# A spectral mixing and ELU kernel: the opening of batch 0 gets own output tiles, fewer early rows and a re-dealt weight conversion

## The chip, the cores and the metric

The kernel runs on one core of a Trainium2 chip. The core has five engines that run their own instruction streams and meet at semaphores: PE (TensorE, matrix multiply), DVE (VectorE), ACT (ScalarE), POOL (GpSimd) and SP (SyncE, which here issues most of the DMAs). The metric is the device time of one launch in microseconds (us).

## The reference

```python
# x (8, 3008, 256), filters (1505, 256), w_in (256, 2048), w_out (2048, 256)
X = np.fft.rfft(x, axis=1)
Y = X * (filt_r + 1j * filt_i)[None]
y = np.fft.irfft(Y, n=3008, axis=1).astype(np.float32)
t = y.reshape(8 * 3008, 256)              # 24064 tokens
h = t @ w_in
g = np.where(h > 0, h, np.exp(np.minimum(h, 0)) - 1)
out = (g @ w_out).astype(np.float32)
```

The two weights and only they come as float64; the kernel makes float32 of them on the chip.

## The kernel before, in words

**Mixing.** 3008 = 47 x 64, so each transform is done as two factors with twiddles inside the tables. Per batch, a first factor (`a_unit`, or `a_first` for batch 0), a second factor with the product by the filter and its inverse (`b_unit`, `bi_unit`; in batch 0 `b_first`, `bi_first`), and a last factor that delivers tokens (`n_unit`, and `n_first` for the first tile of batch 0). Between the second factor and the last the rows pass through a DRAM buffer: `y_write` (`y_write_first`) writes them, `y_read` (`y_read_first`) reads them in another order.

**The two dense layers.** There are 8 x 6 x 4 = 192 items (batch b, token tile m, quarter q of the 2048 hidden columns). An item is 14 up matmuls (`up_steps`, line 592, and the ELU on ACT and DVE) and 14 down matmuls (`down_steps`, line 675); the 2 x 2 block product is done in 7 products, with sums of weight blocks (`w_sums`) and of data blocks (`n_sums`) made ahead. The downs of an item run between the ups of the next. The order of every engine's stream is written by hand: `plan` holds, for a (quad, place) key, what is done in which of five gaps of the loop over items. Batch b+1's mixing units lie in the gaps of batch b's items. Batch 0 runs its items in the order (tile 0: q0, q1), (tile 1: q0 to q3), (tile 0: q2, q3).

**The opening** is what comes before the first item. DMAs bring x, tables, the filter and the first weights (SP in order, some on POOL). `a_first` runs for six x pieces; then for eight tiles g, `t_first` transposes, `b_first` multiplies, DVE makes four `products` with the filter (tile `ff`), and two tiles later `bi_first` does the inverse factor; ACT copies its result from PSUM (lines 388 and 389) into the tile `t3f` for g up to 5, two buffers in turn, and into `t2` for g of 6 and 7. `y_write_first` then sends it to DRAM, 24 rows each. So the copy of tile 2 goes where tile 0's result lies, and has to wait until tile 0's four DMAs have read it. After tile 7 dummy matmuls (`warm`, 5 of them, line 945) run on PE while the rows go out and come back (`y_read_first`, 406) for `n_first` (543). A short burst of such matmuls (3) also stands at the very start.

**Weight conversion.** There are 16 blocks k of 512 float64 values per partition (four per quarter: k%4 of 0 and 1 are w_in, 2 and 3 are w_out). `w_fetch` loads one; `w_split` is two integer operations on DVE (lines 777, 778), `w_float` three activations on ACT (787), `w_join` two more DVE operations (795, 798) and the multiply that writes the weight (802 for w_in, 808 twice for w_out); `w_sums` is four operations on half as many elements, on POOL for most k and on DVE for 13 and 15 (814 to 817). In the opening and in the first six quads these stand between the other work, by the tables `BESIDE` and `early`. An item of quarter q needs the blocks and sums of its quarter before its up or down matmuls.

**Batch 1's first factor** needs sums and differences of x (`x_unit`, 226 and 227): for batch 1 all six pieces on POOL, from batch 2 on DVE. `f_arrange` puts the filter into a DRAM copy `fp`, which `f_read` (POOL's DMA queue, 348) reads per tile; `z_read` and `z_write` pass the first factor's result through DRAM.

Of the kernel before, what the change touches and what calls it, by code (L numbers as in the profile page):

```python
# [37 lines left out]
XSUMS = 6  # L38
WTMP = (0, 1, 0, 1, 0, 1, 2, 3, 0, 2, 3, 2, 3, 2, 3, 2)
# [98 lines left out]
def kernel(  # L138
# [185 lines left out]
    def z_read(b, g):  # L324
        t = t2[:, g % 2]
        for p in range(4):
            k = p * K2 + 4 * g
            nc.sync.dma_start(t[32 * p:32 * p + 24].rearrange("i u d -> i (u d)"),
                              zs[b][:, k:k + 4, :].rearrange("i u d -> i (u d)"))

    def f_read_first(g0, g1, a, queue):

        r = slice(64 * a, 64 * a + 48)
        w0, w1 = 1 if g0 == a == 0 else 0, 2 * (g1 - g0)
        k = 16 * a + 2 * g0
        for c, src in enumerate((filt_r, filt_i)):
            t = ff[r, c, g0:g1].rearrange("p g u d -> p (g u) d")
            queue.dma_start(t[0:48:2], raw(src, k, [[64 * D, 24], [D, w1], [1, D]]))
            for j, n in ((0, 16), (16, 7)):
                queue.dma_start(t[1 + 2 * j:2 * (j + n):2, w0:w1],  # L340
                                raw(src, 64 * (j + 1) - k - w0, [[64 * D, n], [-D, w1 - w0], [1, D]]))
            if w0:
                queue.dma_start(t[1:48:2, 0], raw(src, 32, [[64 * D, 24], [1, D]]))

    def f_read(b, g):
        t = fbufs[g % 2]
        for a in range(4):
            nc.gpsimd.dma_start(t[32 * a:32 * a + 24].rearrange("p c u d -> p (c u d)"),  # L348
                                fp[g, a].rearrange("q c u d -> q (c u d)"))
# [28 lines left out]
    def bi_first(g):  # L378
        s = ss.pop((0, g))
        t = t3s[0, g] = (t2 if g > 5 else t3f)[:, g % 2]  # L380
# [14 lines left out]
    def y_write_first(g, i0=0, i1=24):  # L395
        if g == 0:
# [115 lines left out]
    def n_unit(b, m):  # L512
        t, w, h = t4s.pop((b, m)), tns.pop((b, m)), half(m)
        ps = [bank(n) for n in ("pse", "pso")]
        for q, i in enumerate(order(m)):
            n = 32 if i == 0 else 64
            for dh in range(2):
                for o in (0, 64):
                    for (_, p), r in zip(ps, HALVES):
# [57 lines left out]
    def up_steps(b, m, q):  # L577
# [4 lines left out]
        for tag, names in G_TAGS:  # L582
            t = gp.tile([P, len(names), 2, 256], FP32, tag=tag, name=tag)
# [159 lines left out]
    def w_fetch(k, queue=nc.gpsimd):  # L743
# [4 lines left out]
        elif k in (9, 12):  # L748
            wd = t2[:, 1 if k == 12 else 0].rearrange("p u d -> p (u d)")
        elif k == 13:  # L750
            wd = t3s["first"][:, 0].rearrange("p u d -> p (u d)")
        elif k == 15:
            wd = op.tile([P, 16, 2, 32], FP32, tag="o", name="wd").rearrange("p j e s -> p (j e s)")
        else:
            wd = fbufs[{5: 0, 6: 1, 7: 2, 10: 0, 11: 1, 14: 2}.get(k, k)].rearrange("p c u d -> p (c u d)")
# [33 lines left out]
    def w_join(k, *parts):  # L789
# [3 lines left out]
        for part in parts or range(3):  # L793
# [5 lines left out]
            elif j < 2:  # L799
                a, b = (t.rearrange("p (a j c) -> p a j c", a=2, j=2) for t in (f, e.bitcast(FP32)))  # L800
                dst = w_in[q][:, 2 * j:2 * j + 2, :, :].rearrange("p j a c -> p a j c")
                nc.vector.tensor_tensor(out=dst, in0=a, in1=b, op=ALU.mult)
            else:

                a, b = (t.rearrange("p (i a e s) -> p i e a s", i=2, a=4, e=2) for t in (f, e.bitcast(FP32)))
                dst = w_out[q][:, 0:4, j - 2, :].rearrange("p (i e) (a s) -> p i e a s", i=2, a=4)
                for i in range(2):
                    nc.vector.tensor_tensor(out=dst[:, i], in0=a[:, i], in1=b[:, i], op=ALU.mult)
# [21 lines left out]

    with tc.manual_schedule():


        with tc.tile_pool(name="boot", bufs=1) as bp:
            ff = bp.tile([P, 2, NG, 2, D], FP32, name="ff")
            once = bp.tile([P, 2, P], FP32, name="once")
            eye, gf = once[:, 0], once[:, 1].rearrange("p (v q) -> p v q", v=2)
            gs = bp.tile([P, 3, 2, 64], FP32, name="gs")
            gr, gi = gs[:, 1], gs[:, 2]
# [5 lines left out]
            zt[0] += [bp.tile([P, 16 * ROWS], FP32, name="zt%d" % i) for i in range(2)]  # L845
# [3 lines left out]
            for k in range(3):  # L849
# [7 lines left out]
            for c in range(2):  # L857
                x_load_first(c)
            w_fetch(0, nc.sync)
            for c in range(2, 6):  # L860
                x_load_first(c)
                if c == 3:
                    w_fetch(1, nc.sync)
# [4 lines left out]
            for gh in range(2):  # L868
                nc.gpsimd.memset(ff[:, :, 4 * gh:4 * gh + 4], 0.0)
# [9 lines left out]

            f_read_first(0, 2, 0, nc.sync)  # L880
            f_read_first(0, 2, 1, nc.gpsimd)
            f_read_first(2, 4, 0, nc.sync)
            w_fetch(2, nc.sync)
            f_read_first(2, 4, 1, nc.gpsimd)
            f_read_first(4, 8, 0, nc.sync)
            f_read_first(4, 8, 1, nc.gpsimd)
            ta_first(0)
            ta_first(1)
            w_split(0)
            ta_first(2)  # L890
            ta_first(4)
            for c in range(NXC):
                a_first(c)
                if c == 2:
                    w_float(0)
            w_join(0)
            w_split(1)
            for k in (3, 4):
                w_fetch(k, nc.sync)
            w_fetch(5)  # L900
            t4f = xp.tile([P, 2, 2, D], FP32, tag="xc", name="t4f").rearrange("p k u d -> p (k u) d")
            w_fetch(8)
            t8 = tnp.tile([P, 4, P], FP32, tag="tn", name="t8")
            BESIDE = {0: ((w_float, 1, 0),), 1: ((w_split, 2), (w_float, 1, 1, 2)), 2: ((w_float, 2, 0), (w_join, 1, 0)),
                      3: ((w_join, 1, 1), (w_float, 2, 1, 2)), 4: ((w_join, 1, 2), (w_sums, 1, nc.gpsimd), (w_fetch, 6), (w_split, 3)),
                      5: ((w_join, 2, 0), (w_float, 3, 0)), 6: ((w_join, 2, 1), (w_float, 3, 1, 2)),
                      7: ((w_join, 2, 2), (w_fetch, 7)), 8: ((w_join, 3), (w_split, 4))}
            for g in range(2):
                t_first(g)
            for g in range(NG + 2):  # L910
                back = (lambda g=g: bi_first(g - 2)) if g >= 2 else None
                if g < NG:
                    b_first(g, (ff[:, 0, g], ff[:, 1, g]), pqs[g % 2], back)
# [4 lines left out]
                for fn, *a in BESIDE.get(g, ()):  # L918
                    fn(*a)
                if 2 <= g < NG:  # L920
                    y_write_first(g - 2)
                elif g >= NG:
                    y_write_first(g - 2, 0, 4)
                if g == 4:
                    nc.sync.dma_start(t8, t8_d)
                if g == NG:
                    y_read_first(0, 6)
            y_read_first(6, 8)
            for g in (6, 7):
                y_write_first(g, 4, 24)  # L930
            w_sums(3, nc.gpsimd)
            w_float(4)
            w_split(5)
            w_join(4)
            w_float(5)
            w_split(6)
            w_join(5)
            w_float(6)
            w_sums(5, nc.gpsimd)
            w_split(7)  # L940
            w_join(6)
            w_float(7)
            warm = psO.tile([P, 512], FP32, tag="po2", name="warm")
            for k in range(5):
# [5 lines left out]
        gp = pool("gp", 2)  # L950
        ep = pool("ep", 2)
        op = pool("op", 1)
        n_first(t8)
        tn_read(0, 1)
        y_read(0, 1)
        for k in (9, 10):
            w_fetch(k, nc.sync)
        for c in range(2):
            x_load(1, c)
        for k in (11, 12, 13, 15):  # L960
            w_fetch(k, nc.sync)
# [6 lines left out]
        def at(quad, place, fn, *a):  # L968
            plan.setdefault((quad, place), []).append((fn, a))


        early = ((0, 2, w_join, 7, 0, 1), (0, 2, w_split, 8), (0, 4, w_float, 8, 0), (0, 0, w_float, 8, 1, 2), (0, 0, w_join, 7, 2),
                 (0, 0, w_sums, 7, nc.gpsimd), (0, 3, n_unit, 0, 1), (0, 1, w_join, 8, 0, 1), (0, 1, w_split, 9), (0, 1, w_fetch, 14, nc.sync),
                 (1, 2, n_sums, 0, 1, 0, 1), (1, 2, w_float, 9, 0), (1, 4, n_sums, 0, 1, 2), (1, 0, w_join, 8, 2), (1, 0, w_float, 9, 1, 2),
                 (1, 0, w_split, 10), (1, 3, w_join, 9, 0, 1), (1, 1, w_join, 9, 2), (1, 1, w_sums, 9, nc.gpsimd), (1, 1, w_float, 10, 0),
# [136 lines left out]
```

## Time and profile before

| | us |
|---|---|
| median of 3 runs | 2577.06 (2576.66 to 2580.13) |
| the profiled execution | 2575.46 |
| its span, first to last instruction | 2573.7 |
| PE, DVE, ACT, POOL busy | 2529.4, 2071.6, 1528.2, 189.3 |
| first item's first matmul | 79.73 |
| third item of tile 1 done, seventh item begins | 173.41 |

The profiled execution is 1.6 us below the median. "First item" and "seventh item" are the first matmuls of line 592 of these items in the timeline. The span falls into three parts: the opening, with loads and the first tile's mixing; six items beside which most of the weights are converted; and the rest, about 2400 us, where PE is busy nearly all the time.

### The profile page before, as it was taken

What the parts mean: (1) busy time and instruction counts of PE and PEld (TensorE: products, weight loads), DVE (VectorE), ACT (ScalarE), POOL (GpSimd) and SP (SyncE); (2) the same over time, 40 slices, a digit from 0 to 9 for tenths busy, and PEclk for the clock granted to TensorE, in tenths of its full rate; (3) what the DMA queues carried; (4) which work ended last, traced back from release to release, by engine and by line L of the source; (5) the groups of instructions that cost most, each with busy time, mean ns of one, the idle gap of its engine ahead of it and who ended that gap; (6) DMA issues with size and microseconds to landing.
All of it is one profiled execution on the core that took longest, in us unless ns stands there. A gap on an engine that the chain in (4) does not pass through costs nothing.

```text
span 2573.7 us, 44194 instructions
## 1 busy us (share of the span) xinstructions
PE 2529.4 (98%) x16732; PEld 2160.7 (84%) x16732; DVE 2071.6 (80%) x3612; ACT 1528.2 (59%) x2698; POOL 189.3 (7%) x325
## 2 busy tenths in 40 slices
PE   8889999999999999999999999999999999999998
PEld 5678889888898888988889888888888888898887
DVE  4988887788877888788887888778887788876666
ACT  4665665666556555665556656565656665555554
POOL 3421100010000000000000000000010011000000
PEclk8999999999999999999999999999999999999999
DMA  8753213522234231433215231243213322110010
GB/s 209 207 146 76 68 23 84 138 69 56 48 87 123 56 74 44 113 83 74 61 40 143 71 81 36 72 124 82 56 48 80 85 62 68 36 46 19 19 28 17
DMA packets 229288, 196.38 MB, mean 76 GB/s; under 512 B 129050, under 2 KB 202748, under 8 KB 228980
## 3 DMA queue, kind: packets, MB, share of 16 engines
q1 hardware_dynamic: 215828, 167.62, 26.7%
q0 software_dynamic: 12096, 25.68, 3.5%
q8 instruction: 132, 2.16, 0.3%
q14 instruction: 80, 0.66, 0.1%
q10 hardware_dynamic: 1152, 0.26, 0.1%
HBM read 121.60 MB, written 74.97 MB: 76 GB/s over the span
## 4 chain that ended last, share of the span: by engine, by line
PE 88%; DVE 6%; ACT 2%; DMA 2%; issue 1%; SPq 0%; POOL 0%; DVEq 0%; POOLq 0%; ACTq 0%
PE po L675 41%; PE phs L592 23%; PE phd L592 12%; PE pha L592 6%; PE pse L520 2%; PE pf L419 1%; PE psa L240 1%; PE pv L485 1%; DVE g L600 1%; DVE g L614 1%; DMA ff<-in_filt_i_dram 1%; ACT e L610 1%; ACT e L609 1%; PE pso L520 0%; DMA x<-in_x_dram 0%
## 5 line engine op out<-in xcount | busy, mean ns | idle before, releaser
L675 PE MATMUL po<-g,wo 128*128 128x256 f32 (+1 forms) x5376 | 1316.8, 377 | 0.0
L675 PEld LDWEIGHTS po<-g,wo 128*128 128x128 f32 x5376 | 1013.5, 190 | 165.2 <-issue 49.4
L603 ACT ACTIVATE g<-phs 128x512 f32<-128x512 f32 (+1 forms) x576 | 338.6, 588 | 717.2 <-PE phs L592 716.1
L592 PE MATMUL phs<-y,wi 128*128 128x256 f32 (+1 forms) x2288 | 580.7, 376 | 1.5 <-DVE g L614 1.1
L610 ACT ACTIVATE e<-e 128x512 f32<-128x512 f32 (+1 forms) x768 | 477.1, 621 | 24.3
L592 PEld LDWEIGHTS phs<-y,wi 128*128 128x128 f32 x2288 | 430.5, 190 | 56.5 <-ACT g L603 1.8
L600 DVE TENSOR_TENSOR g<-phd,g 128x512 f32<-128x512 f32 (+1 forms) x384 | 258.9, 674 | 267.0 <-ACT e L610 196.8
L609 ACT ACTIVATE e<-g 128x512 f32<-128x512 f32 (+1 forms) x576 | 353.4, 614 | 66.3 <-DVE g L600 51.2
L614 DVE SCALAR_TENSOR_TENSOR g<-e,g 128x512 f32<-128x512 f32 (+1 forms) x576 | 387.8, 673 | 1.6 <-ACT e L610 0.9
L614 DVE SCALAR_TENSOR_TENSOR g<-e,phs 128x512 f32<-128x512 f32 (+1 forms) x192 | 129.7, 675 | 139.2 <-ACT e L610 139.2
L592 PE MATMUL phd<-y,wi 128*128 128x256 f32 (+1 forms) x768 | 196.3, 378 | 11.4 <-DVE g L600 11.4
L592 PE MATMUL phs<-ys,wi 128*128 128x256 f32 (+1 forms) x784 | 198.7, 376 | 6.4 <-ACT g L603 5.6
L592 PE MATMUL phd<-ys,wi 128*128 128x256 f32 (+1 forms) x768 | 193.8, 375 | 0.0
L592 PE MATMUL pha<-ys,wi 128*128 128x256 f32 (+1 forms) x752 | 190.0, 375 | 0.0
L609 ACT ACTIVATE e<-phs 128x512 f32<-128x512 f32 (+1 forms) x192 | 113.3, 590 | 113.2 <-PE phs L592 113.2
L592 PEld LDWEIGHTS phd<-y,wi 128*128 128x128 f32 x768 | 145.7, 191 | 32.2 <-DVE g L600 16.1
L592 PEld LDWEIGHTS phs<-ys,wi 128*128 128x128 f32 x784 | 147.6, 190 | 25.2 <-ACT g L603 7.8
L348 POOL DMA_DIRECT2D fall<-fp x224 | 110.0, 499 | 692.0 <-DVE r L458 686.4
L592 PEld LDWEIGHTS phd<-ys,wi 128*128 128x128 f32 x768 | 145.7, 190 | 16.6
L592 PEld LDWEIGHTS pha<-ys,wi 128*128 128x128 f32 x752 | 142.8, 190 | 16.5
L600 DVE TENSOR_TENSOR g<-pha,g 128x512 f32<-128x512 f32 (+1 forms) x192 | 129.0, 672 | 24.3 <-PE pha L592 24.3
L654 DVE TENSOR_TENSOR g<-g,g 128x512 f32<-128x512 f32 (+1 forms) x192 | 132.6, 690 | 6.6
(184 smaller groups left out, 2175.4 us busy)
## 6 DMA issues: line engine op xcount, KB each, us to landing
t<-yd SPq DMA_DIRECT2D x94, 256.0 KB
z<-t SPq DMA_DIRECT2D x84, 256.0 KB
fall<-fp POOLq DMA_DIRECT2D x224, 96.0 KB, 2.9
t<-z SPq DMA_DIRECT2D x224, 96.0 KB
yd<-t SPq DMA_DIRECT2D x112, 192.0 KB
out_dram<-o SPq DMA_DIRECT2D x632, 32.0 KB
xc<-in_x_dram SPq DMA_DIRECT2D x84, 128.0 KB
xc<-in_x_dram SPq DMA_DIRECT2D x161, 64.0 KB
```

The lines of the kernel that those rows point to most:

```text
L240: nc.tensor.matmul(p[o:o + 64, u, :], w[r, u, o:o + 64], src[r, u, :], start=True, stop=True)
L348: nc.gpsimd.dma_start(t[32 * a:32 * a + 24].rearrange("p c u d -> p (c u d)"), fp[g, a].rearrange("q c u d -> q (c u d)"))
L419: nc.tensor.matmul(pf[p][1][32 * a:32 * a + 32, js, :], fb[r, v, :], t2[r, js, a, :], start=True, stop=True, tile_position=(32 * p, 32 * a))
L520: nc.tensor.matmul(p[o:o + 64, dh, ds(64 * q, n)], t[r, i - 4 * m, ds(dh * P + o, 64)], w[r, i - 4 * m, 0:n], start=True, stop=True)
L592: nc.tensor.matmul(ps[:, a, 0:h], w_in[q][:, COMBO[n], a, :], y[n], start=start and a == 0, stop=True, skip_group_check=True)
L600: nc.vector.tensor_tensor(out=g[o], in0=i0, in1=i1, op=ALU.add)
L603: nc.scalar.activation(out=g[o], in_=i0, func=AXT.Copy)
L609: nc.scalar.activation(out=e, in_=src, func=AXT.Relu, scale=-1.0)
L610: nc.scalar.activation(out=e, in_=e, func=AXT.Exp, scale=-1.0)
L614: nc.vector.scalar_tensor_tensor(out=g[n], in0=es[n], scalar=1.0, in1=src, op0=ALU.subtract, op1=ALU.max)
L654: nc.vector.tensor_tensor(out=g["t4"], in0=g["b21"], in1=g["t2"], op=ALU.subtract)
L675: nc.tensor.matmul(po[i][:, u, 0:h], w_out[q][:, COMBO[n], a, :], g[n][:, a, :], start=begin and a == 0 and n in (1, 3, 6, 4), stop=True, ...
```

## The change

It has these parts. (1) The filter tile `ff` is split in `ff0` (real) and four tiles `ff1` (imaginary) that lie in the homes of `up_steps`' first g tiles of odd items and of the output tile; the even results of `bi_first` go into those `ff1` tiles, the odd ones into `t3f` and `t2`, so each of the eight results has its own home. POOL clears half as much, ACT clears `ff1`. (2) `y_write_first` sends only the first 8 rows in the opening (4 for tiles 6 and 7, then the other 4), and one `y_read_first` reads them all; rows 8 to 24 are sent during the first items (`early`). (3) The multiply of the conversion becomes `w_mult`, with the engine as an argument; 10 of 16 go to POOL. All conversion steps are single and stand in other places (`OPEN`, `early`); all `w_sums` are on POOL; fetches are all on SP, block 0 ahead of x. (4) `x_unit` of batch 1 runs on POOL for three pieces and on DVE for three. (5) `z_read` and `f_read` move two tiles in one DMA. (6) 6 instead of 3 dummy matmuls at the start and 11 instead of 5 before `n_first`. (7) `n_unit` issues each pair of matmuls in the other order.

```diff
-XSUMS = 6
-WTMP = (0, 1, 0, 1, 0, 1, 2, 3, 0, 2, 3, 2, 3, 2, 3, 2)
+XSUMS = 3
+WTMP = (0, 1, 0, 1, 0, 2, 1, 1, 0, 3, 3, 2, 3, 2, 3, 2)
...
     def bi_first(g):
         s = ss.pop((0, g))
-        t = t3s[0, g] = (t2 if g > 5 else t3f)[:, g % 2]
+        t = t3s[0, g] = outs_first[g]
...
-                    for (_, p), r in zip(ps, HALVES):
+                    for (_, p), r in reversed(tuple(zip(ps, HALVES))):
...
-            t = gp.tile([P, len(names), 2, 256], FP32, tag=tag, name=tag)
+            t = gps[(4 * m + q) % 2].tile([P, len(names), 2, 256], FP32, tag=tag, name=tag)
...
+    def w_mult(k, eng=nc.vector):
+        q, j = divmod(k, 4)
+        _, e, f = w_tmp(k)
+        if j < 2:
...
+            eng.tensor_tensor(out=dst, in0=a, in1=b, op=ALU.mult)
+        else:
...
+            for i in range(2):
+                eng.tensor_tensor(out=dst[:, i], in0=a[:, i], in1=b[:, i], op=ALU.mult)
...
-            ff = bp.tile([P, 2, NG, 2, D], FP32, name="ff")
+            ff0 = bp.tile([P, NG, 2, D], FP32, name="ff")
+            ff1 = [gps[0].tile([P, 2, 2, 256], FP32, tag="g%d" % (i + 1), name="ff") for i in range(3)]
+            ff1.append(op.tile([P, 16, 2, 32], FP32, tag="o", name="ff").rearrange("p (g u w) e s -> p g u (w e s)", g=2, u=2))
+            outs_first = [ff1[g // 2].rearrange("p g u d -> p (g u) d") if g % 2 == 0 else (t3f if g < 4 else t2)[:, g // 2 % 2]
+                          for g in range(NG)]
...
+            OPEN = {0: ((w_split, 1), (w_float, 1, 1, 2, 0),),
...
+                    7: ((w_split, 2), (w_float, 2, 1), (w_fetch, 3, nc.sync), (w_float, 2, 0),),
+                    8: ((w_join, 2, 1), (w_float, 2, 2), (w_join, 2, 0),),
+                    9: ((w_mult, 1, nc.vector), (w_mult, 2, nc.gpsimd),),
...
+                    11: ((w_fetch, 4, nc.sync),),
+                    12: ((w_split, 4), (w_fetch, 7, nc.sync), (w_split, 3),),
...
+                    17: ((w_mult, 3, nc.gpsimd), (w_fetch, 8, nc.sync), (w_split, 9), (w_split, 6), (w_float, 6, 0), (w_split, 5), (w_float, 5, 1, 0), (w_float, 6, 1), (w_join, 6, 1), (w_sums, 3, nc.gpsimd), (w_float, 6, 2),),
+                    18: ((w_join, 6, 0), (w_fetch, 11, nc.sync), (w_join, 5, 1), (w_mult, 6, nc.gpsimd), (w_float, 9, 0), (w_split, 7), (w_float, 5, 2), (w_join, 5, 0),),
+                    19: ((w_fetch, 12, nc.sync),)}
...
-                if 2 <= g < NG:
-                    y_write_first(g - 2)
-                elif g >= NG:
-                    y_write_first(g - 2, 0, 4)
+                conv(8 + g)
+                if g >= 2:
+                    y_write_first(g - 2, 0, 8 if g < NG else 4)
...
+        early = ((0, 2, w_mult, 5, nc.vector), (0, 2, y_write_first, 4, 8, 24), (0, 2, y_read, 0, 1), (0, 2, y_write_first, 6, 8, 24), (0, 2, w_float, 7, 0), (0, 2, y_write_first, 0, 8, 24),
+                 (0, 4, w_float, 7, 1), (0, 4, w_join, 7, 1), (0, 4, w_mult, 4, nc.gpsimd), (0, 4, w_fetch, 10, nc.sync), (0, 4, y_write_first, 2, 8, 24), (0, 4, x_load, 1, 1), (0, 4, w_split, 11), (0, 4, x_load, 1, 0), (0, 4, w_float, 7, 2), (0, 4, w_float, 9, 1),
+                 (0, 0, w_split, 8), (0, 0, x_load, 1, 2),
...
+                 (1, 2, w_float, 8, 1, 0), (1, 2, y_write_first, 5, 8, 24), (1, 2, w_mult, 7, nc.vector), (1, 2, w_float, 8, 2), (1, 2, x_unit, 1, 1), (1, 2, n_unit, 0, 1),
+                 (1, 0, w_join, 8, 0), (1, 0, x_unit, 1, 0), (1, 0, f_arrange, 1, 1), (1, 0, n_sums, 0, 1, 0, 1), (1, 0, w_sums, 7, nc.gpsimd),
...
+                 (4, 3, w_mult, 13, nc.gpsimd), (4, 3, f_arrange, 0, 1), (4, 3, w_mult, 12, nc.gpsimd),
+                 (4, 1, y_read, 0, 2), (4, 1, w_split, 15), (4, 1, w_sums, 11, nc.gpsimd), (4, 1, w_sums, 13, nc.gpsimd),
...
```

## The prediction, made before the changed kernel ran

> **What bounds the kernel now.** I read the page first: PE is busy 98% of the span, so only a stretch where PE is not fed can be shortened. I then asked for busy times by stage, for who waited for whom on PE, and for the timelines of single engines at the places found.
>
> ```profile
> core 0: us, PE busy (x) PEld busy (x) DVE busy (x) ACT busy (x) POOL busy (x), PEclk, DMA share, GB/s
> 46.50:60.00 13.50, 9.71 (x49) 4.14 (x52) 7.20 (x12) 4.77 (x9) 4.09 (x6) 0.62 0.65 202
> 67.10:76.30 9.20, 4.57 (x14) 1.82 (x10) 9.10 (x16) 6.98 (x11) 3.29 (x4) 1.00 0.45 142
> 76.30:80.00 3.70, 3.64 (x17) 3.59 (x18) 3.70 (x5) 2.64 (x5) 3.24 (x4) 0.54 0.62 171
> ...
> 79.70:173.40 93.70, 78.82 (x533) 64.62 (x532) 86.04 (x138) 60.19 (x107) 36.29 (x37) 0.96 0.70 200
> ...
> 484.00:794.00 310.00, 309.78 (x2108) 265.87 (x2098) 255.49 (x447) 186.46 (x330) 18.03 (x36) 1.00 0.31 77
> ```
>
> The last row is a whole batch: PE 309.78 of 310 us, and the batch from 173 to 484 takes 311. So after the seventh item (173.4) nothing that DVE, POOL or a DMA saves is time. Ahead of it are two stages: the opening to 79.73, and six items in 93.7 us where DVE is busy 86.0. PE's waits up to 200 us:
>
> ```profile
> engine line waited for: us in total, times, longest us
> PE phd L592 <- DVE g L600: 7.6, 3, 5.0
> PE phs L592 <- ACT g L603: 5.6, 5, 3.6
> PE psn L543 <- DMA t4f<-yd: 4.7, 1, 4.7
> PE po L353 <- ACT t L388: 3.8, 1, 3.8
> ```
>
> The third and fourth are the opening's: rows that come back late, and ACT's copy of tile 2's result. Why ACT was late, on its timeline (the bracket is idle time before it and what ended it):
>
> ```profile
> 43.42 0.72 ACT L787 ACTIVATE we<-we,edges 128x512 uint32<-128x512 f32 x1
> 50.68 0.60 ACT L388 ACTIVATE t<-po 128x512 f32<-128x512 f32 x1 [6.54 <-DMA yd<-t]
> ```
>
> ACT stood 6.54 us until tile 0's rows had left the buffer. PE then idled 3.8 us and ran at half clock from 49 to 59 (0.62 in the first row above); after its idle of 4.7 us it is at half clock again in `n_first` (0.54).
>
> **Own homes (part 1).** Tile 4's forward matmuls begin at 41.59 and the last inverse matmul ends at 67.11: 25.5 us. At full clock the timeline has 0.91 for a forward step (37.84 to 38.75), 1.02 for a transpose step, and 1.72 for an inverse step (61.86 to 63.58). What remains at 41.59 is 4 forward, 2 transpose and 6 inverse steps: 3.6 + 2.0 + 10.3 = 16.0, so 57.6 if nothing is late. What is late next is DVE: `w_split` 4 and 3 now stand between tile 4's products and tile 5's (four rows of 0.34 start to start, 1.4 us), and tile 5's products also wait until inverse step 3 has read their buffer, which covers about a third. I add 1.3: 58.9, 8.2 us earlier. If block 4's load, which SP issues behind tile 0's writes, lands after 47, its lateness is added: bounds 0 and 4 us.
>
> **Loads ahead of it.** Moving block 0 ahead of x shifts no end: the bytes up to the last x piece are the same, and that piece's landing at 23.7 releases the last `a_first`. Block 2's load goes ahead of the first filter rows: 512 KB at the 235 GB/s of this stretch is 2.2 us; the products begin at 31.14 and wait for PE, the filter's issue ended at 26.1 and would end near 28, so it is covered by about 1 us, and costs 1.2 if the rows land slowly. ACT's four clears end before its first real copy at 11.0. POOL's two clears of 3.5 us become half; they hide under the loads either way.
>
> **Rows out and back (parts 2, 6).** Now 67.11 to 76.36, of which 5 dummies fill 4.56, so 0.91 each. Eleven take 10.0, and PE reaches `n_first` at 68.9. The rows: ACT's last copy ends 1.2 after the last matmul, four issues of 0.35, 2.4 to land (71.4 to 73.9 now), and 2.4 for the read: 7.5, plus block 8's 512 KB that now stands directly ahead on the queue, 2.2: 9.7. The dummies end last, by little. So 10.0 instead of 9.25: +0.8. PE no longer idles there, and `n_first` up to the first item (3.37 us, at half clock) becomes 2.0: -1.4. The opening is 8.2 - 0.8 + 1.4 = 8.8 shorter; the first item starts near 70.9.
>
> **The six items (parts 3, 4).** DVE's operations of 79.7 to 173.4, each at the undisturbed start-to-start time of its shape, sum to 67.7 us; they took 86.0. The rest is this:
>
> ```profile
> 142.64 0.68 DVE L653 TENSOR_TENSOR g<-g,g 128x512 f32<-128x512 f32 x1
> 143.36 1.64 DVE L654 TENSOR_TENSOR g<-g,g 128x512 f32<-128x512 f32 x1
> 144.93 1.75 DVE L795 SCALAR_TENSOR_TENSOR zq<-t,zq 128x512 uint32<-128x512 uint32 x1
> ...
> 143.04 1.41 POOL L226 TENSOR_TENSOR sd<-xc 128x512 f32<-128x512 f32 x1
> 144.53 1.59 POOL L227 TENSOR_TENSOR xc<-xc 128x512 f32<-128x512 f32 x1
> ```
>
> While POOL works on two SBUF operands, a DVE operation of 0.60 takes about 1.67. POOL's elementwise work in the stage is 28.9 us (`x_unit` 19.0, `w_sums` 9.9) and DVE lost 18.3: 0.63 per POOL us. The changed order leaves DVE here 4 instead of 10 multiplies (-6 x 0.66 = -4.0), no sums of 13 and 15 (-3.1), 7 instead of 8 splits (-0.7), and three `x_unit` pairs (+6 x 0.63 = +3.8): 63.7. POOL gets 7 multiplies (512 elements, as `x_unit`: 1.6 each, 11.2), 6 sums (3.2 each, 19.2) and 3 pairs (9.5): 39.9. DVE: 63.7 + 0.63 x 39.9 = 88.8, so +2.8. A multiply moved to POOL thus saves 0.66 and costs about 1.0 wherever DVE has two SBUF operands. DVE's idle time is 7.7 now, 3.8 of it after 161 when it has no conversion left; the new table keeps conversions up to the sixth item, so I take 4.5: -3.2. The first odd item now writes its g tiles where rows 8 to 24 of tiles 0, 2 and 4 lie: its ACT and DVE steps wait for their DMAs. From 63, 28 SP issues at 0.75 (38 in 28.6 us around 95) end at 84, plus 2.4; the last home is needed near 87, the second at 82: I add 1. The stage: +0.6.
>
> [...]
>
> **The rest (parts 5, 7).** Halving POOL's DMA issues (110 us in all) and merging reads lies under a PE that is busy 309.78 of 310: nothing. The new pair order in `n_unit` is on PE's path; the trace does not show it. The entry into an `n_unit` costs 0.09 more than the pitch inside full matmuls (0.31 against 0.22); 47 units of that are 4.2 us, as gain or loss. I take 0.
>
> **Sum.** 8.8 - 0.6 = 8.2 us of the profiled 2575.5, which lies 1.6 under the median; taken off the median of 2577.06: 2568.9. A measurement of this kernel can tell about 0.2%, 5.2 us, from no change.
>
> **The rivals.**
> 1. *POOL gives the gain back* (0.15). DVE stands nearly still while POOL works: 1.07 lost beside a POOL row of 1.41 is 0.76 per us, and DVE keeps its 7.7 us idle. The stage is 63.7 + 30.3 - 86.0 = +8.0, and +1 for the homes: 2577.1 - 8.8 + 9.0 = 2577.3. For it: the three rows above. Against: PSUM readers (line 600) stay at 0.60 beside POOL, and 0.63 is the stage's mean. [...]
> 2. *SP falls behind, and POOL's in-order queue with it* (0.15): the slower side. POOL's `x_unit` 1 and 0 now stand ahead of the sums of block 7 and the multiply of 9, and wait for x loads that are SP's 40th issue after 63. At 0.75 each they land at 95 and sums 7 end at 102, about when the third item's downs need them, so from there each us is a us of PE. At 1.17 per issue (nine in 10.5 us from 13.21, with large loads in flight) it is 16.8 later, less 2 of slack: 2577.1 - 8.8 + 14.8 = 2583. For it: 16 late row writes ahead of those loads. Against: they are small, 64 KB.
> 3. *The homes do not help fully* (0.08): block 4's or the filter's landing replaces the wait, 4 us of the 8.2 are lost: 2573.
> 4. *The stage shrinks too* (0.10): POOL's sums and multiplies fall beside PSUM readers and DVE's need falls to 63.7 + 18.3: -4.0 - 3.2 + 1 = -6: 2562.
>
> **How the numbers follow.** The forecast has 0.52, with its own range 2564 to 2573. Faster by over 0.2% (below 2571.9): 0.48 of the forecast, all of rival 4, a fifth of 1 and a quarter of 3 at their lower ends: about 0.63. Slower by over 0.2% (above 2582.2): most of rival 2, 0.13. The rest is 0.24. The range, 2560 to 2581, takes in rivals 1, 3, 4 and the mild end of 2, and the bound of `n_unit`.
>
> **What would show it.** Right: no ACT wait for yd<-t at the copy, clock 1.00 from 46 to 60, last inverse matmul near 59, `n_first` straight after the eleven dummies, the first item near 71, seventh near 165. The stage's DVE busy near 89 with POOL near 40. Wrong: a PE wait in the second item ended by a yd DMA, sums of 7 ending after 102, DVE waiting for block 4's DMA at tile 5, or a batch that no longer takes 310.

## The result, and the profile after

| | before | after |
|---|---|---|
| median, six runs each on the same chip | 2578.68 (2576.66 to 2580.13) | 2562.84 (2562.08 to 2566.71) |
| profiled execution | 2575.46 | 2562.93 |
| its span | 2573.7 | 2560.8 |
| last inverse matmul ends | 67.2 | 57.6 |
| first item begins | 79.73 | 69.91 |
| items one to six | 93.7 | 84.9 |
| seventh item | 14.1 | 19.4 |
| eighth item begins | 187.47 | 174.24 |
| thirty-first item to the last down matmul | 2081.3 | 2081.3 |

The ratio of the times is 0.9942, with a 95% interval of 0.9929 to 0.9955: the change is faster, by 0.6%. The forecast was 2568.9, 6.1 us above the median, inside its range of 2560 to 2581, on the side that had 0.63, but below the forecast's own range of 2564 to 2573. The last row says where the difference is not: every kernel of this study, with or without any part of the change, has 2081.3 to 2081.5 there, the kernel before with its own pair order and single reads among them. All is decided before the eighth item: 9.8 us in the opening and 8.8 in six items are gained, and 5.4 are given back in the seventh.

The busy times by stretch of the changed kernel, as those of the prediction (us; busy time of each engine and its instructions, granted clock, DMA share, GB/s):

```profile
core 0: us, PE busy (x) PEld busy (x) DVE busy (x) ACT busy (x) POOL busy (x), PEclk, DMA share, GB/s
46.50:60.00 13.50, 13.50 (x110) 5.46 (x103) 12.13 (x21) 9.64 (x18) 2.95 (x3) 1.00 0.73 223
...
69.90:154.80 84.90, 76.71 (x535) 63.79 (x533) 79.33 (x123) 61.01 (x109) 43.44 (x45) 0.98 0.80 217
154.80:174.20 19.40, 17.79 (x108) 13.28 (x101) 15.22 (x27) 10.05 (x22) 3.79 (x4) 0.87 0.64 163
470.80:780.80 310.00, 309.78 (x2105) 265.96 (x2097) 255.60 (x447) 186.46 (x330) 11.60 (x20) 1.00 0.34 77
```

From 46.5 to 60 PE is busy throughout at full clock (9.71 us at 0.62 before). In the six items POOL works more than before and DVE less. The seventh item, which before was 14.1 us of PE at clock 1.00, is 19.4 us at 0.87. A batch still takes 310. The waits of PE up to 200 us:

```profile
engine line waited for: us in total, times, longest us
PE phs L591 <- ACT g L602: 5.2, 6, 2.3
...
PE phd L591 <- DVE g L599: 3.2, 3, 1.5
...
PE pf L418 <- DMA t<-z: 1.6, 3, 0.7
PE psn L542 <- DMA t4f<-yd: 0.8, 1, 0.8
```

The waits for DVE are 3.2 in place of 7.6 us, the longest 1.5 in place of 5.0. That for the rows that come back is 0.8 instead of 4.7. New is the wait of `b_unit` (line 418) for batch 1's `z`. On ACT's timeline the copies of results no longer wait for a row write, only for PE:

```profile
47.94 0.60 ACT L387 ACTIVATE t<-po 128x512 f32<-128x512 f32 x1 [1.70 <-PE po L352]
51.69 0.60 ACT L387 ACTIVATE ff<-po 128x512 f32<-128x512 f32 x1 [1.18 <-PE po L352]
```

PE's timeline at the end of the opening: the dummies start behind the last inverse matmul, `n_first` is at full clock (2.00 us for its 16 matmuls).

```profile
57.55 9.71 PE L966 MATMUL warm<-wi 128*128 128x512 f32 x22
68.08 2.00 PE L542 MATMUL psn<-t,t4f 128*128 128x128 f32 x16 [0.81 <-DMA t4f<-yd]
```

### The profile page after: what moved, and what is told of

It is laid out like the page before. It is cut to its first block, busy times and chain, and to the rows that moved or that the text cites. A ratio compares the mean times of both kernels' runs of the same rounds, so it can differ in the third digit from the quotient of the medians.

```text
span 2560.8 us, 43958 instructions
## 1 busy us (share of the span) xinstructions
PE 2531.4 (99%) x16750; PEld 2160.8 (84%) x16750; DVE 2064.2 (81%) x3594; ACT 1530.4 (60%) x2702; POOL 154.3 (6%) x230
## 4 chain that ended last, share of the span: by engine, by line
PE 90%; DVE 5%; DMA 2%; ACT 2%; issue 1%; SPq 0%; DVEq 0%
PE po L674 42%; PE phs L591 24%; PE phd L591 12%; PE pha L591 6%; PE pf L418 2%; PE pso L519 2%; PE psa L240 1%; PE pv L484 1%; DVE g L599 1%; DVE g L613 1%; DMA z<-t 0%; ACT e L609 0%; PE po L352 0%; ACT e L608 0%; PE psa L291 0%
## 5 line engine op out<-in xcount | busy, mean ns | idle before, releaser
L674 PEld LDWEIGHTS po<-g,wo 128*128 128x128 f32 x5376 | 1014.5, 190 | 165.5 <-issue 49.9
L591 PEld LDWEIGHTS pha<-ys,wi 128*128 128x128 f32 x752 | 142.9, 190 | 16.5
L650 DVE TENSOR_TENSOR g<-g,g 128x512 f32<-128x512 f32 (+1 forms) x192 | 132.0, 687 | 6.7
L653 DVE TENSOR_TENSOR g<-g,g 128x512 f32<-128x512 f32 (+1 forms) x192 | 131.1, 683 | 6.6
```

The lines of the kernel that those rows point to most:

```text
L591: nc.tensor.matmul(ps[:, a, 0:h], w_in[q][:, COMBO[n], a, :], y[n], start=start and a == 0, stop=True, skip_group_check=True)
L650: nc.vector.tensor_tensor(out=b12, in0=b22, in1=b12, op=ALU.subtract)
L653: nc.vector.tensor_tensor(out=g["t4"], in0=g["b21"], in1=g["t2"], op=ALU.subtract)
L674: nc.tensor.matmul(po[i][:, u, 0:h], w_out[q][:, COMBO[n], a, :], g[n][:, a, :], start=begin and a == 0 and n in (1, 3, 6, 4), stop=True, ...
```

## The experiments

"Changed" is the kernel after the change. The columns of this table are start times and lengths in the profiled executions (us), and the timed median with its ratio to the kernel before, taken on the same chip. The rows come from several chips (the kernel before had medians of 2576.9 to 2579.7 on them), so two rows are compared by their ratios, not by their medians.

| | last inverse ends | item 1 begins | items 1 to 6 | item 7 | item 8 begins | median | ratio, 95% |
|---|---|---|---|---|---|---|---|
| before | 67.2 | 79.73 | 93.7 | 14.1 | 187.47 | 2578.68 | |
| changed | 57.6 | 69.91 | 84.9 | 19.4 | 174.24 | 2562.84 | 0.9942 [0.9929, 0.9955] |
| e1 old homes | 61.5 | 76.81 | 85.4 | 15.7 | 177.94 | 2566.16 | 0.9948 [0.9933, 0.9963] |
| e2 rows now | 59.3 | 76.29 | 84.9 | 14.8 | 176.02 | 2565.15 | 0.9948 [0.9932, 0.9965] |
| e3 multiplies on DVE | 57.8 | 70.08 | 84.5 | 18.8 | 173.33 | 2561.68 | 0.9935 [0.9920, 0.9950] |
| e4 z first | 57.9 | 69.63 | 85.4 | 14.4 | 169.43 | 2559.80 | 0.9925 [0.9911, 0.9940] |
| e5 before, own homes | 60.1 | 73.44 | 96.2 | 14.1 | 183.70 | 2574.24 | 0.9981 [0.9972, 0.9990] |
| e6 before, 3 x units | 69.4 | 83.64 | 93.9 | 14.1 | 191.55 | 2577.27 | 0.9990 [0.9981, 0.9999] |
| e7 z first, multiplies on DVE | 60.1 | 71.46 | 84.7 | 18.3 | 174.48 | 2562.81 | 0.9935 [0.9918, 0.9952] |
| e8 five dummies | 58.7 | 72.03 | 86.0 | 18.9 | 176.96 | 2565.59 (one run) | |
| e9 old shares | 57.9 | 70.51 | 91.1 | 17.2 | 178.78 | 2567.48 | 0.9956 [0.9942, 0.9969] |
| e10 order of pairs | 59.3 | 70.80 | 85.4 | 19.2 | 175.41 | 2562.55 | 0.9934 [0.9921, 0.9948] |
| e11 z first, mixed | 57.6 | 70.45 | 84.9 | 14.4 | 169.72 | 2558.35 | 0.9918 [0.9905, 0.9932] |
| e12 six x units on POOL | 58.3 | 70.54 | 90.0 | 14.4 | 174.89 | 2564.20 | 0.9952 [0.9936, 0.9969] |

How far a profile can be read: the seven kernels that have the changed opening but for multiplies and order (e3, e4, e7, e9 to e12) begin item 1 at 69.63 to 71.46, and the two that have the old opening (before, e6) at 79.73 and 83.64. So one start has about 2 us of play after the change and about 4 before it. Part of the play after the change has a name: at tile 5 DVE waits for block 4's load, 1.1 us in the changed kernel and 1.4 to 3.7 in the ten others with the new load order, and where it waits 3.2 us or more (e2, e7, e10) the last inverse matmul ends at 59.3 to 60.1. The changed kernel's 57.6 is near the lucky end.

### Homes and rows

**e1**, the first two parts undone:

```diff
-        t = t3s[0, g] = outs_first[g]
+        t = t3s[0, g] = (t2 if g > 5 else t3f)[:, g % 2]
...
-                    y_write_first(g - 2, 0, 8 if g < NG else 4)
+                    y_write_first(g - 2, 0, 24 if g < NG else 4)
```

The late `y_write_first` entries are gone, and the read of rows is two again.

> The changed kernel with the first two parts undone: results go home where they did before the change, all their rows are written in the opening, the late row writes leave the items; the dealing of the conversion stays. Theory (the opening's 9.8 us come from the homes): ACT waits for yd<-t again, half clock returns ahead of 60 us, last inverse matmul near 66 instead of 57.6, first item near 79; the seventh item loses some of its 19.4 us, since 32 row writes leave SyncE's queue during the items, so the end is 2566 to 2573. Rival (the opening's gain comes from the conversion's new dealing there, not from the homes): first item still near 70, end 2557 to 2563.

The ACT waits came back, on its timeline:

```profile
47.02 0.60 ACT L387 ACTIVATE t<-po 128x512 f32<-128x512 f32 x1 [4.33 <-DMA yd<-t]
50.95 0.60 ACT L387 ACTIVATE t<-po 128x512 f32<-128x512 f32 x1 [1.87 <-DMA yd<-t]
```

But the last inverse matmul ended at 61.5, not 66: half clock lasted only 3.4 us there, against 10.2 before the change. The first item began at 76.81, not near 79; that is 6.9 later than in the changed kernel, and the seventh item fell to 15.7. The end is in the expected range.

**e2**, own homes, all rows at once (only the two `y_write_first` calls of the opening get 24 as their end, and the late entries go):

> The changed kernel with own homes kept, but all 24 rows of each result written in the opening and none late. Tells homes from late rows. If the homes alone give the opening's gain: last inverse matmul at 57 to 59 as in the changed kernel, clock 1.00 from 46 to 60, and only the landing of the read of rows moves, by up to 5 us (1.5 MB more go ahead of it), so the first item is at 70 to 75; SyncE has 32 fewer issues (about 0.65 us each) in the items, so batch 1's z comes earlier and the seventh item falls from 19.4 towards 14. End 2558 to 2566. Rival (late rows are what gives the gain): first item near 79.

A miss of the expectation's first item. The homes did their part (59.3), but the rows came late. PE's timeline:

```profile
72.82 3.68 PE L542 MATMUL psn<-t,t4f 128*128 128x128 f32 x16 [3.89 <-DMA t4f<-yd]
```

The read is issued at 68.36 instead of 64.24 and lands 4.7 later; PE idles 3.9 us behind the dummies and `n_first` runs at half clock, 3.68 against 2.00. The first item begins 6.4 us later than in the changed kernel. At least 4.7 of it is the rows; the other 1.7 stand already in the last inverse's end, and e10 shows the same 59.3 with late rows. But the seventh item is 14.8 when no rows are left for it: 4.6 of the 6.4 go back there.

**e5**, the reverse: the kernel before with one line changed.

```diff
-        t = t3s[0, g] = (t2 if g > 5 else t3f)[:, g % 2]
+        t = t3s[0, g] = ff[:, 1, g:g + 2].rearrange("p g u d -> p (g u) d") if g % 2 == 0 else (t3f if g < 4 else t2)[:, g // 2 % 2]
```

> The kernel before with own homes for the opening's results and nothing else changed: all 24 rows are written in the opening, the conversion keeps its old dealing and POOL its old share. The prediction gave the homes 8.2 us by themselves (last inverse matmul 67.11 to 58.9): then the clock is 1.00 from 50 us on, the last inverse matmul starts at 58 to 60, and since the whole rows still go ahead of the read (it landed 13.6 us after the last inverse matmul in the kernel with own homes and whole rows) the first item is near 75 to 77 instead of 79.73, end 2574 to 2576. Theory from the kernel with old homes under the new dealing (last inverse matmul at 60.4): the homes are only part of it, the old dealing and old load order hold the opening too, the last inverse matmul starts at 62 to 66 and the first item at 77.5 to 79.7, end 2576 to 2579.

The stretch from 46.5 to 60, and the start of `n_first`, in two views of this kernel:

```profile
46.50:60.00 13.50, 13.33 (x105) 4.51 (x97) 13.13 (x23) 7.31 (x13) 5.18 (x8) 1.00 0.82 259
```

```profile
70.00 3.65 PE L543 MATMUL psn<-t,t4f 128*128 128x128 f32 x16 [5.45 <-DMA t4f<-yd]
```

The homes alone bring the clock to 1.00 and the last inverse matmul from 67.2 to 60.1: 7.1 of the forecast 8.2 us. The first item was even earlier than expected (73.44), since the rows landed at 70.0. Part of the 7.1 is play ahead of the homes. From tile 4's first forward matmul to the end of the last inverse one it is 25.6 us before (25.9 in e6, which has the same opening), 19.8 in e5, 19.9 in e1 and 16.3 in the changed kernel (18.1 in e10). So homes alone give about 6 us, and the new dealing and load order alone (e1) give about 6 as well; together they give 7 to 9, not 12. The same stall goes away by either. The six items became 96.2, so at the eighth item 3.8 are left of 6.3.

**e8**, 5 dummies in place of 11 before `n_first`:

> The changed kernel with 5 dummy matmuls instead of 11 ahead of the first step of the first item. Theory (the dummies cost nothing, as the rows read back land at 68.1 anyway, and they hold the clock): the wait for t4f<-yd grows from 0.81 to about 6 us, the clock falls to a half, the first step's 16 matmuls take 3.6 us instead of 2.0, first item at 71.5 instead of 69.9. Rival (the dummies themselves hold the rows' work back): first item at 69 or earlier.

```profile
68.57 3.67 PE L542 MATMUL psn<-t,t4f 128*128 128x128 f32 x16 [5.38 <-DMA t4f<-yd]
```

As the theory had it: the wait grows to 5.4, the clock is 0.50 from 66.3 on, and the first step takes 3.67. The first item begins at 72.03: the six extra dummies save 1.7 us of half clock, and the rows come no earlier without them.

### The six items

The six items are two halves that behave differently. This table cuts them at the fourth item's first matmul and gives the length of each half and DVE's busy time in it (us, from the windows of each profile).

| | items 1 to 3 | DVE busy | items 4 to 6 | DVE busy |
|---|---|---|---|---|
| before | 43.2 | 40.1 | 50.5 | 45.9 |
| e5 before, own homes | 45.5 | 40.1 | 50.7 | 46.0 |
| e6 before, 3 x units | 45.5 | 39.1 | 48.4 | 43.8 |
| changed | 41.0 | 37.3 | 43.9 | 42.0 |
| e3 multiplies on DVE | 40.6 | 36.8 | 43.9 | 41.8 |
| e9 old shares | 40.0 | 37.2 | 51.1 | 46.0 |
| e12 six x units on POOL | 40.1 | 38.3 | 49.9 | 44.6 |

The other kernels with the new order (e1, e2, e4, e7, e8, e10, e11) have 40.4 to 42.1 in the first half and 43.9 to 44.1 in the second (45.0 in e4). So the first half has about 2 us of play, and the second stands firm.

**e3**, all ten `w_mult` of POOL with `nc.vector`:

> The changed kernel with all ten multiplies on DVE instead of POOL (three of them in the opening). The prediction's rule (a multiply on POOL saves 0.66 us of DVE and costs about 1.0 beside it): the six items get 2 to 3 us shorter, end near 2560.5. Theory from the changed kernel's trace (a multiply on POOL costs DVE only 0.17 to 0.19 of its own length there, some 0.25 us): DVE gets seven multiplies of 0.66 back and loses seven times 0.25 of stretch, the six items get about 3 us longer (84.9 to about 88), end near 2566.

Both numbers missed. Six items took 84.5, the same within the play. The same stretch as in the changed kernel's second row above:

```profile
70.10:154.60 84.50, 76.88 (x535) 64.30 (x534) 78.61 (x128) 60.28 (x108) 31.84 (x33) 0.98 0.82 219
```

POOL has 11.6 us less to do: six multiplies that begin in the window (10.3) and the end of block 4's. DVE has six more multiplies in this window (0.68 each by the groups of instructions, 4.1) and yet is busy 0.7 less. So beside POOL these multiplies had cost DVE 4.8, 0.41 of POOL's time. But DVE's busy time in the first half differs by 1 us and more between kernels with the same shares; in the firm second half the same working gives 2.9 lost for 10.1 us of POOL, 0.29. So the rate is 0.3 to 0.4, and a multiply on POOL saved 0.68 and cost 0.5 to 0.8: no gain and no loss that these runs can tell. The 0.17 to 0.19 of my reading of the changed kernel's overlaps was too small. And the seventh item now waits for the last quarter's weights:

```profile
PE po L674 <- DVE wo L813: 2.7, 1, 2.7
```

**e6**, the kernel before with `XSUMS = 3`:

> The kernel before with three of batch 1's six x units on DVE instead of POOL, one constant changed. In its trace POOL's x units cost DVE 12.0 us for 19.0 us of POOL work (0.63 per us). Theory (taking x units off POOL is a large part of what shortened the six items from 93.7 to 84.9): three units give back about 6 us of stretch and cost six sums of 0.60 (3.6 us), so DVE's busy time in the six items falls by about 2.4 us, and the stage and the end with it, 2576 to 2577. Rival (which engine does it is of no account, the new order of the single steps is): stage 93 to 95, end 2578 to 2580.

```profile
83.60:177.50 93.90, 79.84 (x534) 65.82 (x534) 82.87 (x141) 60.30 (x107) 25.26 (x29) 0.94 0.70 200
```

DVE's busy time fell by 3.2 (2.4 expected), from 86.0, and the six items did not get shorter: 93.9. Taken as a whole this looks like the rival, but the halves say otherwise. The first x unit that moved runs on DVE at 134, after the third item's end at 129.1. Behind it items 4 to 6 fell by 2.1 (50.5 to 48.4), as DVE's busy time there did (45.9 to 43.8), and PE's waits for DVE fell by 2.1 in all (7.6 to 5.5). The first half grew by 2.3 before the edit could act, just as in e5, which leaves the x units alone; both have 6.8 us of half clock there, the kernel before 3.4 (mean clock of the six items 0.94 in both, 0.96 before). By the medians the kernel is 2.4 us faster (ratio 0.9990, the interval just below 1), the size that the theory had. So the theory holds, and the profiled execution, the slowest of ten, hid it. By items 4 to 6 the x units cost DVE 0.63 per us of POOL (DVE 2.2 less with six more operations of 0.63, for 9.5 us of POOL), the rate that the forecast had used.

What holds the first half in the old order is another queue. DVE, ACT and PE in the kernel before:

```profile
96.55 1.48 DVE L777 TENSOR_SCALAR zq<-t 128x512 uint32<-128x512 uint32 x1
98.06 0.63 ACT L787 ACTIVATE zq<-zq 128x512 f32<-128x512 uint32 x1 [5.13 <-DVE zq L777]
99.18 1.02 PE L592 MATMUL phs<-ys,wi 128*128 128x224 f32 x4 [3.59 <-ACT g L603]
```

A `w_float` on ACT (787) waits 5.1 us for its `w_split` (777), which DVE reaches late; the copy (603) that PE needs stands behind it in ACT's stream, and PE waits 3.6 us (5.6 in e5 and e6). In the changed kernel PE's longest wait in this half is 2.3.

**e9**, old shares in the new order (`XSUMS = 6`, all multiplies and the sums of 13 and 15 on DVE):

> The changed kernel with the engines' old shares in the new order: all six x units of batch 1 on POOL, all multiplies on DVE, the sums of blocks 13 and 15 on DVE, as before the change; the order of single steps and everything else stays new. Tells what shortened the six items from 93.7 to 84.9: the shares or the order. If the order: the six items stay at 84 to 88 us, first item near 70, end 2561 to 2567 (the seventh item keeps the 18.8 that it had with the last multiplies on DVE). If the shares: the six items go back to 91 to 94, end 2568 to 2572.

Six items took 91.1, which is the expectation's "shares" range. The halves are plainer: the first has the new order's length (40.0), the second the old one's (51.1, before 50.5). So the order of steps, with all else that is new, shortens items 1 to 3 (by 1 to 5.5 us, given the play of both sides), and the shares shorten items 4 to 6, by 7.2 under the new order.

**e12**, only the x units back on POOL:

> The changed kernel with one constant back: all six x units of batch 1 on POOL. Under the old order of steps moving three of them to DVE left the six items at 93.9; under the new order, all old shares together gave 91.1 against 84.9. This run tells which of the old shares costs it. If the x units: items four and five (18.7 and 18.7 with all old shares, 15.3 and 14.2 in the changed kernel) grow to 17 to 19 each, the six items are 89 to 91, end 2566 to 2568. If it was the sums of blocks 13 and 15 on DVE: the six items stay at 84 to 86, end 2562 to 2564.

```profile
70.50:160.50 90.00, 78.18 (x535) 64.96 (x533) 82.86 (x117) 60.81 (x109) 52.27 (x51) 0.96 0.81 221
```

The six items took 90.0, the fourth 16.5 and the fifth 20.4. With six operations fewer (0.63 each, 3.8) DVE is busy 3.5 more, for 8.8 us more of POOL: 0.83 lost per POOL us, or 0.61 by items 4 to 6 (2.5 more, for 10.3). So of the 7.2 that the old shares cost, the x units are 6.0, more than the 2.1 that three of them cost under the old order. In the fifth item (a window from 127 to 147.5) stands a stall of the kind above:

```profile
ACT zq L786 <- DVE zq L776: 5.5, 1, 5.5
...
PE phs L591 <- ACT g L602: 4.3, 1, 4.3
```

But the end is hardly later (2.6 us by the ratios, whose intervals overlap): the seventh item took 14.4 instead of 19.4, and the eighth began at 174.89, beside 174.24. What the six items gained was given back in the seventh.

### Where the seventh item's time went

SP's timeline in the changed kernel, the last writes of batch 1's `z` and its first read:

```profile
149.53 1.30 SPq L322 DMA_DIRECT2D z<-t  x2
...
157.73 1.25 SPq L322 DMA_DIRECT2D z<-t  x2
...
163.03 1.54 SPq L327 DMA_DIRECT2D t<-z  x4
```

The last matmuls of that first factor (line 240) had started by 139, yet SP issues the last write at 157.73. Between them stand late rows, the filter's rearrangement, reads of rows and the loads of batch 2's x. The read at 163.03 comes 8 us into the seventh item. In e3 it is issued at 161.8 and in e12 at 162.2, though DVE and POOL have other work there.

**e4** puts four loads of batch 2's x (20 issues) behind that read:

```diff
-                        at(t + s, 1, x_load, nb, nxt)
+                        at(*((6 + c // 4, 1) if b == 1 and c > 1 else (t + s, 1)), x_load, nb, nxt)
```

> The changed kernel with four loads of batch 2's x (20 issues on SyncE) put behind the first read of batch 1's z instead of ahead of it. Theory (the seventh item's 5.4 us are a late z: SyncE issues z's last write 18 us after the matmuls that make it): last z write near 146 instead of 158, z read near 152 instead of 163, no PE wait for t<-z in the seventh item, clock 1.00 in it, item 14 to 15 us instead of 19.4; end near 2557.5. Rival (batch 1's first forward step is late through something else, or its late start was what kept DVE free): the seventh item stays over 18 us, or a later one grows by as much; end 2562 to 2563.

SP's timeline and the seventh item's window:

```profile
140.10 3.25 SPq L322 DMA_DIRECT2D z<-t  x4
...
147.59 1.54 SPq L327 DMA_DIRECT2D t<-z  x4
```

```profile
155.00:169.40 14.40, 14.33 (x108) 11.85 (x101) 14.13 (x24) 9.19 (x19) 4.33 (x5) 1.00 0.70 169
```

The read comes 15 us earlier, no `t<-z` wait is left, the clock is 1.00, the item 14.4. The eighth begins 4.8 earlier, and the span is 2556.3, 4.5 less; by the ratios the gain is 4.4, though the two intervals overlap. The theory of the late z is shown in the trace.

**e7** (e4, all multiplies on DVE, the fourth set's row read an item later) and **e11** (e4, only the multiplies of 4 and 10 on DVE):

> Candidate for a version faster than both: the changed kernel with the loads of batch 2's x behind z's read, the read of the fourth set of rows an item later, and all multiplies on DVE. If the two effects add (z first: the seventh item 19.4 to 14.4, 4.7 us by the profile; multiplies on DVE: 0.5 us of the six items, 0.4 of the seventh): item 8 begins near 168.5 against 174.24, end 2557 to 2559. If multiplies on DVE gained only because z was late: end 2559 to 2561, no better than z first alone.

> Candidate for a version faster than both: the changed kernel with the loads of batch 2's x behind z's read, and of the multiplies only blocks 4 and 10 on DVE. With all multiplies on DVE items one, two and four were 2.9 us shorter together and the third 2.3 longer, and the seventh waited 2.7 us for a late weight of the fourth quarter; with only 4 and 10 on DVE the first two gains should stay and the seventh item stay at 14.4. If so: eighth item near 167 to 168, end 2556.5 to 2559. Rival (a multiply on DVE only shifts the wait to the next item): eighth item near 169.4 as with z first alone, end 2559 to 2560.

e7 did not add up: its seventh item took 18.3 with z in time, because the downs waited 2.7 us for the multiply of line 813 on DVE and 1.0 for the sums behind it. Where the multiplies run matters there, not in the six items. e11 kept the 14.4, but the first two items' gain came back as a longer third (19.2); its eighth item begins at 169.72, no earlier than in e4: the rival. Its ratio to the kernel before, 0.9918, is the lowest of all (changed 0.9942), so it is the best candidate for a version that beats both; but the changed kernel was not timed beside it, the two intervals overlap a little, and its profile is no better than e4's.

### The order of pairs

**e10**, `reversed(...)` taken out of `n_unit`:

> The changed kernel with the pairs of matmuls of the shift step in the order that they had before the change. The prediction put this edit at 0 with bounds of 4.2 us either way over the whole run; the batches' length is the same before and after (the end is 2069 us after the thirty-first item's start in the old order and in the new). Expected: no difference, end 2561 to 2565, every batch as long as in the changed kernel. Rival (the order of the pairs hides or shows a weight load): each of the 24 steps moves by up to 0.17 us, the end by up to 4.2.

No difference: a ratio of 0.9934 beside 0.9942, and 2081.3 us from the thirty-first item to the last down matmul, as everywhere (the 2069 of the expectation is a slip for this number).

## Why the prediction was right, point by point

**Own homes**: right. Forecast 58.9 for the end of the last inverse matmul, measured 57.6; homes alone, in e5, 60.1. DVE did wait for block 4 at tile 5, which the prediction had named as a sign of being wrong: 1.07 us here, up to 3.7 in the other runs, within the bound of 0 to 4. In the nine other kernels with own homes and the new order the end lies at 57.6 to 60.1. What the step had not seen is that the new dealing and load order would have removed most of the same stall by themselves (e1).

**Rows out and back**: right. `n_first` was forecast for 68.9 and began at 68.08, at full clock; the rows, not the dummies, ended last, by 0.8. The first item was forecast for 70.9 and began at 69.91. The opening: 8.8 forecast, 9.8 measured.

**The six items**: this is the step that failed: +0.6 forecast, 8.8 shorter measured. The way was wrong too, as the forecast let the stage grow. Most of its inputs were good: POOL's elementwise work 38.8 (39.9 forecast), DVE's operations at their undisturbed times 64.1 by my count (63.7), DVE's idle time 5.6 (4.5). The rate was not: DVE was busy 79.3 instead of 88.8, so it lost about 15 us beside 38.8 of POOL, 0.39 per us instead of 0.63. The rate before was mostly that of x units (19.0 of POOL's 28.9 us; e6 gives the same 0.63 for them alone), and the forecast gave it to multiplies and sums too; multiplies cost 0.3 to 0.4 (e3), and for sums no run tells it. The sentence that a multiply on POOL saves 0.66 and costs about 1.0 does not hold: it cost 0.5 to 0.8, which is even. The 1 us for homes that are still being read did not come: neither ACT nor DVE waits for a row write in items 1 to 3.

The model behind the step, a stage as DVE's sum plus a little idle time, held in one half only. In items 4 to 6 the length followed DVE's sum in e6 (2.1 and 2.2), and in the changed kernel 3.9 of the 6.6 are DVE's and 2.7 are idle time that went. In items 1 to 3 the old order held PE behind ACT's queue, which the forecast counted nowhere; that half became 2.2 shorter here. How much the sums of 13 and 15 bring no run tells by itself.

**The rivals.** The fourth (the stage shrinks too, 2562) was nearest in its number: DVE's need was put at 82.0 and was 79.3. Its cause, POOL's sums and multiplies falling beside steps that they do not hold up, fits the low rate but was not tested by a run. The first (POOL gives the gain back, 0.76 per us) is against the measured 0.39. The second was right in mechanism and wrong in place: SP did fall behind through late row writes, but at batch 1's z in the seventh item (3.7 us of it by e1, 4.6 by e2), not at the x loads of the second; the sums of block 7 ended at 97.5, ahead of the 102 that it had named. The third was there in part, as block 4's wait. The forecast took the batch after the sixth item as fixed and had no term for the seventh.

Per us of POOL's work DVE lost 0.63 us to the x units in e6, 0.61 to 0.83 to them in e12, and 0.3 to 0.4 to the multiplies in e3: each time less than POOL's own time.

**The rest**: right, nothing: 2081.3 to 2081.5 in every kernel. Nor did the new loads and dummies at the start show: tile 4's first forward matmul begins at 41.31, before at 41.59.

Over all: the opening was right to 1 us, the stage wrong by 9.4, the seventh item unforeseen by 5.4 the other way. That the total stayed inside the range is luck: without the seventh item's 5.4 the median would have been near 2557.5, below it. So 13.2 us at the eighth item instead of 8.2; the medians are 15.8 apart, 2.6 more than the item starts, because the profiled execution of before lies 3.2 below its median here.

## What to carry to other kernels

Do not judge a run by a stage's total: cut the stage where the edit begins to act. In e6 the total stood still, because a half that the edit could not reach had grown by as much as the other half gained. A stage is the busy sum of its fullest engine only where no queue's order holds the work up; ask of each half which it is. A rate of disturbance measured on one kind of work is not the rate of another (here 0.63 per us of POOL for x units in e6, 0.3 to 0.4 for multiplies in e3). Follow the gain to the next meeting point of engines: what is won ahead of a transfer that an in-order queue issues at its own pace can be given back there (here 5.4 us), and the cheapest gain can be to issue that transfer ahead of loads nobody needs yet (4.4 us by the ratios in e4). Two edits may remove the same stall; undo each alone, and do each alone, before crediting either.

## What the runs showed of the hardware

In the traces of the kernel before and of the changed kernel, apart from the last stretch of each run, which the end of the run cuts off, half clock (0.50) came in nine stretches, each of 3.4, 6.8 or 10.2 us. In the 3.4 us ahead of each of them PE was busy for 0.2 to 2.2 us. One came after a short wait: in the changed kernel PE idles 2.28 us ahead of 97.12 and is at half clock just after.

```profile
97.12 1.45 PE L591 MATMUL phs<-ys,wi 128*128 128x256 f32 x3 [2.28 <-ACT g L602]
```

```profile
97.40:100.70 3.30, 3.30 (x10) 2.77 (x10) 3.27 (x6) 0.60 (x1) 0.15 (x1) 0.50 0.84 250
```

So this wait of 2.3 us cost, by my estimate (half of the 3.4 us at half clock that followed), 1.7 us more than itself. Idle time alone does not tell when: of two stretches of 3.4 us, the one in the changed kernel from 165.6, with PE busy for 2.2 us, was followed by half clock, and the one in the kernel before from 131.2, with 1.4 us, was not (1.00 from 134.6 to 137.9); what decides stays open. Two kernels that differ little can differ in it: the profiled execution of e4 has a mean clock of 0.998 and 1.00 in the seventh item, that of the changed kernel 0.996 and 0.87, with two stretches of half clock between 23 us and its last one, 10.2 us in all.
